# Gathers of expert passes issued one pass at a time, behind small VectorE copies of their row numbers

## The chip, the cores and the metric

The kernel runs on one core of a Trainium2 chip. Its time is the device time of one execution in microseconds (us). Three timed runs of the kernel before gave 411.81, 412.93 and 413.04 us, a median of 412.93.

## The reference

The program is an attention block followed by a mixture of experts.

```
state = f[:, :, t, :, None] * state + einsum('bhd,bhe->bhde', k[:, :, t], v[:, :, t])
y[:, :, t] = einsum('bhd,bhde->bhe', q[:, :, t], state)        # f = sigmoid(f_logit), 768 steps
x = y.transpose(0, 2, 1, 3).reshape(3072, 384)
g = argmax(x @ w_group);  e = argmax(x @ w_expert[g])          # 4 groups x 4 experts
out[token] = softmax(group)[g] * softmax(expert)[e] * (relu(x @ w1[g, e]) @ w2[g, e])
```

The sizes are batch 4, 8 heads, 768 steps, head width 48; 3072 tokens of 384 values; 16 experts with a hidden width of 1024. All is float32. A token goes to one expert only, so the kernel must find the tokens of each expert before it can multiply them.

## The kernel before

**Attention and routing** fill the first 144 us or so. They write each token's row of 384 values, with its weight and its number (386 values, 1544 bytes), to `x_dram` in HBM, and make two tables on VectorE (DVE): `rows_p` (L338), the token numbers of the 16 expert passes, and `who`, the expert of each pass.

**The expert passes** follow, 16 of them, in the order of `PLACES`. Pass 0 and the last one take 128 tokens, the fourteen between take 230 down to 174 (`WIDTHS`), the large experts first; two "early" passes of 128 tokens each are worked in between the end of attention. For a pass the kernel does this:

- `pass_of` calls `fetch` (L399 to L405), which issues the gathers of its rows from `x_dram`: an indirect DMA of up to 128 rows each, from GpSimd's (POOL's) queue, one for a pass of 128 tokens and two for a wider one. The target `xg` has six buffers.
- The rows must be turned so that the 384 values lie along the partitions. For the wide passes `square_in` does it with 16 32x32 block transposes on DVE (L426), into one of two `xe` buffers. For passes of 128 tokens, and for pass 1 at the start, `turn_in` does it on TensorE (PE, L440), and DVE copies the result from PSUM to `xe` (L441).
- `up` multiplies by w1 on PE (`hp`, L450), and ScalarE (ACT) applies relu into `h` (L451).
- `down` multiplies by w2 (`yo`, L471 for 128 tokens, L486 for wider ones). A wide pass's result is turned back by `square_out` on DVE (L433), scaled on ACT, and scattered to the output by an indirect DMA from POOL's queue (L461) that reads the token numbers from `xg`.

The weights of a pass, two loads of 1.5 MB, are issued from SP's queue (L392) and follow the release of weight buffers, three passes ahead.

**What sets the order.** In iteration n of the main loop (L964 on), PE runs `up` of pass n + 1 and then `down` of pass n. DVE runs `square_out` of pass n - 1, then `square_in` of pass n + 2. The program's order is kept on PE, DVE, ACT and SP. POOL's order is the scheduler's choice, by its own estimate of when each instruction is ready.

**The start.** At L940 `pass_of` is called for passes 0, 1 and 2, and each iteration n calls it for pass n + 3 at its beginning. As nothing but a free `xg` buffer and `rows_p` holds a gather back, the scheduler puts the first six passes' gathers (1 + 5 x 2 = 11) in a row on POOL's queue. PE meanwhile finishes the early passes' `yo` (L471), and turns in passes 0 and 1 between the steps of `up` of pass 0 (L955 to L963).

Of the kernel before, what the change touches and what calls it, by code (L numbers as in the profile page):

```python
# [12 lines left out]
U32 = mybir.dt.uint32  # L13
# [5 lines left out]
P = 128  # L19
# [4 lines left out]
def kernel(  # L24
# [12 lines left out]
    nc = tc.nc  # L37
# [5 lines left out]
    GE = G * EG  # L43
# [8 lines left out]
    EARLY = 2  # L52
    CLOSE = NC - 3

    WIDTHS = (230, 222, 214, 212, 208, 204, 200, 196, 193, 191, 189, 186, 182, 174)
# [21 lines left out]
    def const(shape, dtype, name):  # L77
        return cp.tile(shape, dtype, tag=name, name=name)

    def bank(shape, name):  # L80
        return ps.tile(shape, FP32, tag="bank", name=name)
# [192 lines left out]
    rows_p = const([P, GE, 2], U32, "rows_p")  # L274
# [120 lines left out]
    def load_weights(pool, ap):  # L395
        e = value(ap, GE - 1)
        return load_layer(pool, e, 1), load_layer(pool, e, 2)

    def fetch(pool, rows, n, top=N, late=False):  # L399

        w = {"n": n, "pool": pool, "early": top < N, "late": late, "blocks": [(j, min(P, n - j * P)) for j in range((n + P - 1) // P)]}
        w["x"] = pool.tile([P, len(w["blocks"]), RW], FP32, tag="xg", bufs=2 if pool is ep else 6, name="xg")
        for j, m in w["blocks"]:
            nc.gpsimd.indirect_dma_start(out=w["x"][:, j, :], out_offset=None, in_=x_dram[0:1 + top, :], in_offset=bass.IndirectOffsetOnAxis(ap=rows[:, j:j + 1], axis=0))  # L404
        return w  # L405

    def room(w, shape, name):

        full = w["pool"].tile([P, shape, P if w["pool"] is ep else WIDE], FP32, tag=name, name=name)
        w[name[:2].replace("xe", "xT") + "_full"] = full  # L410
        return full[:, :, 0:w["n"]]

    def squares(w, turn):


        for k_ in range(P // SQ):
            n = sum(j * P + k_ * SQ < w["n"] for j, m in w["blocks"])
            for g in range(P // SQ):
                turn(n, k_, slice(k_ * SQ, (k_ + 1) * SQ), g, slice(g * SQ, (g + 1) * SQ))

    def square_in(w):

        w["xT"] = room(w, KO, "xe")
        x = w["x"][:, :, 0:DM].rearrange("p j (o g c) -> p j g o c", o=KO, c=SQ)
        xT = w["xT_full"].rearrange("p o (j k c) -> p j k o c", j=2, c=SQ)
        squares(w, lambda n, k_, rk, g, rg: nc.vector.transpose(out=xT[rg, 0:n, k_], in_=x[rk, 0:n, g]))  # L426

    def square_out(w):

        w["rows"] = w["pool"].tile([P, 2, DM], FP32, tag="yr", name="yr")  # L430
        y = w["rows"].rearrange("p j (o g c) -> p j g o c", o=KO, c=SQ)
        yT = w["yT_full"].rearrange("p o (j k c) -> p j k o c", j=2, c=SQ)
        squares(w, lambda n, k_, rk, g, rg: nc.vector.transpose(out=y[rk, 0:n, g], in_=yT[rg, 0:n, k_]))  # L433

    def turn_in(w):
        w["xT"] = room(w, KO, "xe")
        for j, m in w["blocks"]:
            pt = bank([P, KO, P], "xg_ps")
            for ko in range(KO):
                nc.tensor.transpose(out=pt[:, ko, 0:m], in_=w["x"][0:m, j, ko * P:(ko + 1) * P], identity=ident[0:m, 0:m])  # L440
            (nc.scalar.copy if w["early"] else nc.vector.tensor_copy)(w["xT"][:, :, j * P:j * P + m], pt[:, :, 0:m])  # L441
# [34 lines left out]
    def down(w, w2):  # L476
        n = w["n"]
        if n == P:
            for _ in down_rows(w, w2):
                pass  # L480
            return
        w["yT"] = w["yT_full"][:, :, 0:n]
        for m in range(KO):
            yp = bank([P, n], "yo")
            for fo in range(FO):
                nc.tensor.matmul(yp, lhsT=w2[:, fo, m * P:(m + 1) * P], rhs=w["h"][:, fo, :], start=(fo == 0), stop=(fo == FO - 1))  # L486
            nc.scalar.copy(w["yT"][:, m, :], yp)  # L487

    def scaled(w, settle=False):
        if w["n"] > P:  # L490
            for j, m in w["blocks"]:
                with settled(settle and j):
                    put(w, j, m, w["rows"][:, j, :])
# [414 lines left out]
    mo = main.enter_context(tc.tile_pool(name="mo", bufs=2))  # L908


    PLACES = [0] + list(range(EARLY, GE)) + list(range(1, EARLY))

    def pass_of(n):
        p = PLACES[n]
        if p < EARLY:
            return fetch(mo, rows_p[:, p, 1:2], P)
        return fetch(mo, rows_p[:, p, :], WIDTHS[p - EARLY])

    fari = const([1, 1], I32, "fari")

    def weakest():

        worst = const([P, 1], FP32, "worst")
        nc.vector.tensor_reduce(out=worst, in_=decays.rearrange("p c a n -> p (c a n)"), axis=AX, op=OP.min)
        wt = bank([1, P], "wt")
        nc.tensor.transpose(out=wt, in_=worst, identity=ident)
        far = const([1, 2], FP32, "far")
        nc.vector.tensor_reduce(out=far[:, 0:1], in_=wt, axis=AX, op=OP.min)
        nc.vector.tensor_scalar(far[:, 1:2], far[:, 0:1], math.exp(-SAFE), None, OP.is_lt)
        nc.vector.tensor_copy(fari, far[:, 1:2])  # L930

    def flags():

        nc.vector.tensor_copy(both[:, 0:1], fari)
        nc.vector.tensor_scalar(rest, b_end, 0, None, OP.is_gt)
        nc.vector.tensor_tensor(both[:, 1:2], fari, rest, OP.max)

    both = const([1, 2], I32, "both_i")
    rest = const([1, 1], I32, "rest")
    ws = {n: pass_of(n) for n in range(3)}  # L940
    ahead = {n: load_weights(wq if n % 3 == 1 else wp, who[0:1, PLACES[n]:PLACES[n] + 1]) for n in range(1, 2)}
    ahead[0] = weights[0]

# [6 lines left out]
    def run_up(n):  # L950
        for _ in up(ws[n], ahead[n][0]):
            pass
# [6 lines left out]
    next(opening)  # L959
    next(opening)  # L960
    turn_in(ws[1])
    for _ in opening:
        pass  # L963
    for n in range(GE - 1):  # L964
        w = ws[n]
        if n + 3 < GE:
            ws[n + 3] = pass_of(n + 3)
        if n == 0:
            ahead[2] = load_weights(wp, who[0:1, PLACES[2]:PLACES[2] + 1])
        past, coming = ws.pop(n - 1, None), ws.get(n + 2)  # L970
        if past and past["n"] > P:
            square_out(past)
        if coming and coming["n"] > P:
            square_in(coming)
        if n + 2 < GE:
            run_up(n + 1)
        if past:

            scaled(past, n == GE - 3)
        if coming and coming["n"] == P:  # L980
            turn_in(coming)
        w["yT_full"] = outs[n % 2]
        down(w, ahead.pop(n)[1])
        if n + 3 < GE:
            ahead[n + 3] = load_weights(wq if n % 3 == 1 else wp, who[0:1, PLACES[n + 3]:PLACES[n + 3] + 1])
        if n == 2:
            with tc.tile_pool(name="tb", bufs=1) as tb:
                beyond(False, tb)
        if n == 3:
            weakest()  # L990
            flags()
# [79 lines left out]
    with tc.If(more > 0), ExitStack() as late:  # L1071
# [3 lines left out]
        mo = late.enter_context(tc.tile_pool(name="mo2", bufs=2))  # L1075
# [49 lines left out]
```

## Time and profile before

| What | us |
|---|---|
| timed runs, median of three | 412.93 |
| the profiled execution's own time | 417.84 |
| its span, first to last instruction | 416.0 |
| PE busy | 404.0 |
| DVE busy | 264.3 |
| ACT busy | 162.2 |
| POOL busy | 85.7 |

The mean granted clock of PE was 0.994 of full speed. In the views of the profile, a line of the chain or of a timeline begins with the start and the length in us; L450 is line 450 of the kernel; `out<-in` are the names of the tiles; a bracket gives the engine's idle time ahead of the group and what ended it. POOL's span of an indirect DMA is the issuing, not the transfer. PE's matmuls are pipelined and their ends are modelled.

### The profile page before, as it was taken

Reading aid. Unit: us, or ns where it says so; the run is one execution under the profiler, and the core shown is the slowest. Engines: PE = TensorE matmul, PEld = TensorE weight load, DVE = VectorE, ACT = ScalarE, POOL = GpSimd, SP = SyncE. Lnnn points to the kernel's source line nnn. Section 1 sums busy time; section 2 is a strip of 40 time slices with the busy share of each in tenths; the row PEclk is TensorE's granted clock in tenths of the full one; section 3 lists DMA queues with packets and bytes.
Section 4 is the critical chain, followed back from the end, with each engine's and each line's share of the span. In section 5 each row is a group of like instructions: output and inputs, shape, how many; then the busy total and the mean of one; then the engine's idle time right before and its main releaser. Section 6 shows DMA issues by size and latency. Waiting matters only on the chain.

```text
span 416.0 us, 10268 instructions
## 1 busy us (share of the span) xinstructions
PE 404.0 (97%) x4143; PEld 371.9 (89%) x4143; DVE 264.3 (64%) x783; ACT 162.2 (39%) x365; POOL 85.7 (21%) x132
## 2 busy tenths in 40 slices
PE   8999999999999997999999999999999999999994
PEld 3888888888888966989999999999999999999992
DVE  6666878787998702440799767485595595584230
ACT  6777878887664211211223122222231232232220
POOL 5000010101040174001041221311321230120230
PEclk9999999999999999999999999999999999999999
DMA  9999987879869499855729467586495596485010
GB/s 191 208 216 197 201 179 147 164 159 289 244 225 378 163 337 345 318 179 184 271 84 335 137 245 265 164 315 208 170 348 169 217 352 200 173 318 162 28 48 24
DMA packets 132146, 88.99 MB, mean 214 GB/s; under 512 B 102582, under 2 KB 122748, under 8 KB 132090
## 3 DMA queue, kind: packets, MB, share of 16 engines
q1 hardware_dynamic: 125666, 75.50, 60.6%
q0 software_dynamic: 5792, 11.92, 9.5%
q10 hardware_dynamic: 632, 0.83, 0.6%
q8 instruction: 35, 0.57, 0.6%
q14 instruction: 21, 0.17, 0.1%
HBM read 78.71 MB, written 9.83 MB: 213 GB/s over the span
## 4 chain that ended last, share of the span: by engine, by line
PE 48%; issue 30%; DMA 9%; POOL 6%; DVE 3%; POOLq 1%; another core or an unknown queue 1%; ACT 1%; SPq 0%; ACTq 0%; DVEq 0%
PE hp L450 12%; PE yo L486 6%; DMA out_dram<-yt,xg 6%; PE yo L471 4%; PE cs L616 4%; POOL out_dram L461 4%; PE ap L704 3%; PE y L746 3%; POOL xg L404 2%; PE x_ps L795 2%; PE tr_q L650 2%; PE tr_k L650 2%; PE y L742 2%; PE ap L689 2%; PE y L754 2%
## 5 line engine op out<-in xcount | busy, mean ns | idle before, releaser
L450 PE MATMUL hp<-xe,w 128*128 128x128 f32 (+14 forms) x864 | 141.3, 323 | 2.6 <-issue 1.8
L450 PEld LDWEIGHTS hp<-xe,w 128*128 128x128 f32 x864 | 137.4, 192 | 4.5 <-issue 2.4
L486 PE MATMUL yo<-h,w 128*128 128x230 f32 (+13 forms) x672 | 115.8, 333 | 0.0
L433 DVE STREAM_TRANSPOSE yr<-yT 32x192 f32<-32x192 f32 (+1 forms) x208 | 70.5, 339 | 70.5 <-ACT yT L487 67.9
L486 PEld LDWEIGHTS yo<-h,w 128*128 128x128 f32 x672 | 113.7, 190 | 0.2
L451 ACT ACTIVATE h<-hp 128x256 f32<-128x256 f32 (+14 forms) x72 | 34.2, 478 | 109.1 <-PE hp L450 100.2
L426 DVE STREAM_TRANSPOSE xe<-xg 32x192 f32<-32x192 f32 (+1 forms) x208 | 69.6, 335 | 8.7 <-PE hp L450 5.8
L461 POOL DMA_INDIRECT out_dram<-yt,xg x32 | 34.5, 1078 | 156.1 <-ACT yt L458 150.5
L487 ACT COPY yT<-yo 128x230 f32<-128x230 f32 (+13 forms) x42 | 13.5, 325 | 80.5 <-PE yo L486 80.5
L404 POOL DMA_INDIRECT xg<-x_dram,rows_p x30 | 29.6, 986 | 51.1 <-DMA out_dram<-yt,xg 25.7
L471 PE MATMUL yo<-w,h 128*128 128x384 f32 x64 | 21.3, 486 | 0.0
L707 DVE TENSOR_TENSOR am<-ap,tri 128x512 f32<-128x512 f32 x24 | 15.1, 688 | 7.3 <-PE ap L704 7.3
L616 PE MATMUL cs<-ld_f,tri 128*128 128x384 f32 x48 | 18.5, 505 | 0.5 <-POOL blank L177 0.3
L471 PEld LDWEIGHTS yo<-w,h 128*128 128x128 f32 x64 | 11.9, 190 | 7.4
L458 ACT ACTIVATE yt<-yr,xg 128x384 f32<-128x384 f32 (+13 forms) x26 | 14.4, 604 | 5.4 <-DVE yr L433 5.4
L623 POOL DMA_DIRECT2D ends<-eq x10 | 5.4, 542 | 52.2 <-ACT eq L617 52.2
L692 DVE TENSOR_TENSOR am<-ap,seen 128x384 f32<-128x384 f32 x24 | 12.2, 551 | 5.5 <-PE ap L689 5.5
L757 ACT COPY xT<-y 128x512 f32<-128x512 f32 x24 | 13.4, 587 | 5.0 <-PE y L746 4.4
L651 ACT COPY Tk<-tr_k 128x512 f32<-128x512 f32 x24 | 15.2, 636 | 0.0
L651 ACT COPY Tq<-tr_q 128x512 f32<-128x512 f32 x24 | 15.0, 625 | 0.4 <-PE tr_q L650 0.3
L441 DVE COPY xe<-xg_ps 128x384 f32<-128x384 f32 (+1 forms) x4 | 2.1, 535 | 20.5 <-remote 9.7
L650 PE MATMUL tr_q<-ident,qh 128*128 128x128 f32 x96 | 14.5, 274 | 0.5 <-issue 0.5
(187 smaller groups left out, 448.4 us busy)
## 6 DMA issues: line engine op xcount, KB each, us to landing
w<-in_moe_w_dram SPq DMA_DIRECT2D x34, 1536.0 KB, 7.2
qh<-in_q_dram SPq DMA_DIRECT2D x12, 384.0 KB, 6.1
ld_k<-in_k_dram SPq DMA_DIRECT2D x12, 384.0 KB, 4.4
v<-in_v_dram SPq DMA_DIRECT2D x12, 384.0 KB, 5.4
ld_f<-in_f_logit_dram SPq DMA_DIRECT2D x11, 384.0 KB, 5.5
x_dram<-x_kept SPq DMA_DIRECT2D x2, 1536.0 KB
x_dram<-x POOLq DMA_DIRECT2D x2, 384.0 KB
x_dram<-x ACTq DMA_DIRECT2D x2, 384.0 KB, 7.4
```

The source lines that it names most:

```text
L404: nc.gpsimd.indirect_dma_start(out=w["x"][:, j, :], out_offset=None, in_=x_dram[0:1 + top, :], in_offset=bass.IndirectOffsetOnAxis(ap=rows ...
L426: squares(w, lambda n, k_, rk, g, rg: nc.vector.transpose(out=xT[rg, 0:n, k_], in_=x[rk, 0:n, g]))
L433: squares(w, lambda n, k_, rk, g, rg: nc.vector.transpose(out=y[rk, 0:n, g], in_=yT[rg, 0:n, k_]))
L450: nc.tensor.matmul(hp[:, o, :], lhsT=w1[:, ko, (f + o) * P:(f + o + 1) * P], rhs=w["xT"][:, ko, :], start=(ko == 0), stop=(ko == KO - 1))
L451: nc.scalar.activation(h[:, f:f + 2, :], hp, AF.Relu)
L461: sent = nc.gpsimd.indirect_dma_start(out=out, out_offset=bass.IndirectOffsetOnAxis(ap=w["x"][0:m, j, DM + 1:RW].bitcast(U32), axis=0), in ...
L471: nc.tensor.matmul(yp, lhsT=w["h"][:, fo, :], rhs=w2[:, fo, :], start=(fo == 0), stop=(fo == FO - 1))
L486: nc.tensor.matmul(yp, lhsT=w2[:, fo, m * P:(m + 1) * P], rhs=w["h"][:, fo, :], start=(fo == 0), stop=(fo == FO - 1))
L616: nc.tensor.matmul(cs.rearrange("t h d -> t (h d)"), lhsT=tri, rhs=nl[:, b], start=True, stop=True)
L650: nc.tensor.transpose(out=pt[:, a, :], in_=w[nm + "h"][:, b, 2 * a:2 * a + 2, :].rearrange("t r d -> t (r d)"), identity=ident)
L651: nc.scalar.copy(w["T" + nm][:, b], pt)
L707: nc.vector.tensor_tensor(am[:, r], ap[r], tri.unsqueeze(1).broadcast_to((P, HP, P)), OP.mult)
```

## The change

A new constant tile `rows_next` has the shape of `rows_p`. For every pass after the second, `pass_of` first has DVE copy the pass's row numbers (128 partitions x 2) from `rows_p` to `rows_next`, and the gathers read them from there. A gather therefore waits for a DVE copy that stands in DVE's program order. The calls are also placed later: pass 2's after the turning in of pass 1, and pass n + 3's after `square_in` of pass n + 2 instead of at the start of the iteration.

```
+    rows_next = const([P, GE, 2], U32, "rows_next")
     def pass_of(n):
         p = PLACES[n]
+        if n > 1:
+            nc.vector.tensor_copy(rows_next[:, p, :], rows_p[:, p, :])
         if p < EARLY:
-            return fetch(mo, rows_p[:, p, 1:2], P)
-        return fetch(mo, rows_p[:, p, :], WIDTHS[p - EARLY])
+            return fetch(mo, (rows_next if n > 1 else rows_p)[:, p, 1:2], P)
+        return fetch(mo, (rows_next if n > 1 else rows_p)[:, p, :], WIDTHS[p - EARLY])
...
-    ws = {n: pass_of(n) for n in range(3)}
+    ws = {n: pass_of(n) for n in range(2)}
...
     turn_in(ws[1])
+    ws[2] = pass_of(2)
     for _ in opening:
         pass
     for n in range(GE - 1):
         w = ws[n]
-        if n + 3 < GE:
-            ws[n + 3] = pass_of(n + 3)
...
         if coming and coming["n"] > P:
             square_in(coming)
+        if n + 3 < GE:
+            ws[n + 3] = pass_of(n + 3)
```

In the built program POOL's queue is then: the gathers of passes 0 and 1 (three), the two clearings of `yT`, the outputs of the two early passes, the gathers of passes 2, 3 and 4, the output of pass 0, and from there on the two gathers of a pass and the outputs of an earlier one in turn. On DVE the fourteen copies stand behind the `xe` copies of pass 1 and then behind each `square_in`. The order of the instructions on PE, ACT and SP is the same as before.

## The prediction

> **What bounds the kernel now.** I read the page's busy table first, then the chain that ended last, then the timelines of the three engines that the change touches, then the windows around it.
>
> ```profile
> span 416.0 us, 10268 instructions
> PE 404.0 (97%) x4143; PEld 371.9 (89%) x4143; DVE 264.3 (64%) x783; ACT 162.2 (39%) x365; POOL 85.7 (21%) x132
> ```
>
> PE is busy for 404.0 of 416.0 us, so whatever does not reach PE is worth nothing. The moved gathers are on POOL (21%) and the new copies on DVE (64%), neither of them the bound. The question is where PE is not fed. The chain over 150 to 200 us shows the one place in the expert part:
>
> ```profile
> 154.90 2.68 PE hp L450 x24
> 157.57 0.64 PE xg_ps L440 x6
> ...
> 158.36 0.39 ACT h L451
> 158.75 4.46 another core or an unknown queue
> ...
> 163.23 0.94 ACT h L451 x3
> ...
> 164.32 11.24 PE hp L450 x48
> 175.56 5.16 PE yo L471 x16
> 180.72 9.00 PE hp L450 x48
> ```
>
> After 180.72 the chain is PE without a gap. Before it stands a hole of 4.46 us that no queue explains. It falls inside POOL's burst:
>
> ```profile
> 144.72 1.02 POOL L404 DMA_INDIRECT xg<-x_dram,rows_p  x1 [4.43 <-ACT h L451]
> 146.05 0.99 POOL L404 DMA_INDIRECT xg<-x_dram,rows_p  x1 [0.30 <-issue]
> 147.34 0.95 POOL L404 DMA_INDIRECT xg<-x_dram,rows_p  x1 [0.30 <-issue]
> 148.59 0.95 POOL L404 DMA_INDIRECT xg<-x_dram,rows_p  x1 [0.30 <-issue]
> ...
> 157.98 0.95 POOL L404 DMA_INDIRECT xg<-x_dram,rows_p  x1 [0.30 <-DMA xg<-x_dram,rows_p]
> 159.23 1.02 POOL L461 DMA_INDIRECT out_dram<-yt,xg  x1 [0.30 <-issue]
> ```
>
> Eleven gathers go out from 144.72 to 157.98, one each 1.25 us, and two outputs behind them. The trace's semaphore records say when they land: the first 6.5 us after its issue, the eighth to eleventh 8.9 to 9.1 us. Only the first three (passes 0 and 1) are needed soon. The windows, with columns PE, PEld, DVE, ACT, POOL busy, clock, DMA share, GB/s:
>
> ```profile
> 152.00:158.00 6.00, 6.00 (x41) 4.89 (x41) 0.56 (x1) 0.58 (x1) 4.48 (x6) 1.00 1.02 331
> 158.00:164.30 6.30, 3.70 (x26) 2.98 (x25) 1.02 (x3) 1.32 (x4) 2.96 (x3) 1.00 1.02 338
> 164.30:181.00 16.70, 16.68 (x67) 13.99 (x68) 10.55 (x31) 2.46 (x5) 0.00 (x0) 0.90 0.65 249
> ```
>
> In 158 to 164.3 the DMA engines are full, PE works 3.70 of 6.30 us, and afterwards PE's clock is 0.90 of full. The last view is DVE's timeline:
>
> ```profile
> 163.28 0.94 DVE L441 COPY xe<-xg_ps 128x384 f32<-128x384 f32 x2 [9.67 <-remote]
> 164.14 5.70 DVE L426 STREAM_TRANSPOSE xe<-xg 32x192 f32<-32x192 f32 x16
> 175.60 5.71 DVE L426 STREAM_TRANSPOSE xe<-xg 32x192 f32<-32x192 f32 x16 [5.76 <-PE hp L450]
> ```
>
> The copies of pass 1 wait with PE; the transposes of pass 2 start at once, at 164.14, as their rows have long been there. This is what the change takes away.
>
> [...] in 158 to 164 us the gathers' queue takes 47.9% and the weights' queue 54.2% of the engines. [...] half clock for 3.41 us from 164.9. [...]
>
> **The change, part by part.**
>
> *Removed from 148 to 159 us:* eight gathers of 128 rows of 1544 bytes, 1.6 MB, and 8 x 1.25 = 10 us of POOL's queue. What the hole costs: PE could have gone on after the transposes of 157.41 to 158.0 with the 24 records of hp left to pass 0, at 0.112 us each (2.68 us for 24 in the chain), so pass 1 could start at about 160.8 instead of 164.32: 3.5 us. Half clock for 3.41 us costs another 1.7 us, which agrees with 11.24 us for pass 1's 48 records against 9.00 x 230/222 = 9.3 us. Together 5.2 us. Taken away whole, the profiled execution's own 417.84 us (span 416.0 and 1.84 around it) would be 412.6. The median of the timed runs is already 412.93, 4.9 below the profiled execution. So either the hole is absent from timed runs, or it is in them and the 4.9 us are profiling cost of another kind. Lower bound of the gain 0, upper bound 5.2 us. I take half, 2.7, as likeliest value where there is a gain[...].
>
> *Added: 14 copies* of 128x2 row numbers on DVE. The nearest row is the cast that makes row numbers, 0.18 us for 128x32. 14 x 0.18 = 2.5 us over 230 us, one per pass. They hide in DVE's wait for PE's results: 4.3 to 5.3 us in every pass from the sixth on. Without that cover they would cost 0.2 us a pass. In passes 2 and 3 DVE has no such gap (it goes from 199.54 to 231.6 unbroken); there the transposes for pass 5 end at 231.32, and PE needs them at 233.95. Three copies add 0.5: still hidden.
>
> *Moved: the gathers of pass 2.* They now wait for a DVE copy behind the copies of pass 1 and, on POOL, stand behind the two early outputs, whose rows ACT finishes at 150.0 and 155.5, so these do not hold them. With the hole gone, pass 1's copies end at about 159.1; copy and semaphore 0.5, first gather 1.3, so the second is issued at 160.9. It must land, then come 5.7 us of transposes, and pass 2 starts on PE at 160.8 + 9.4 + 5.2 = 175.4. Room for landing: 175.4 - 5.7 - 160.9 = 8.8 us. Gathers of the trace under full DMA took 6.4 to 8.0 us where no burst stood ahead. Margin about 1 to 2 us, the narrowest of the change. If the hole stays, the margin is similar: copies end 164.2, second gather at 166.0, room 180.6 - 5.7 - 166.0 = 8.9.
>
> *Pass 3:* its copy follows pass 2's transposes (about 174.7), the second gather goes at 176.5, lands by 184.5, transposed by 190.2, needed at 175.4 + 9.0 + 9.3 = 193.7. *Pass 4:* issued at 191 to 192, landed by 200; its transposes stand behind pass 1's output transposes until 199.5 anyway. *Later passes:* a gather goes out after the previous pass's input transposes and is used one period (15 to 17.5 us) less those 5.7 us later; with 2 us of issue and 7 to 8 us to land it is there 1 to 2 us before DVE asks, and DVE itself is 4 to 5 us ahead of PE.
>
> *POOL's queue behind the new wait:* the output scatters of a pass now stand behind gathers that wait for DVE; they go 2 to 4 us later (output 0 about 9 us later). Nobody waits: four output buffers, six gather buffers. In return POOL no longer waits for the scatters to land (25.7 us in 7 waits), which PE never saw. SP's weight loads keep their places; they share the engines with 1.6 MB less until 165 us. The last gather is before 380 us and the final scatters keep their order, so the tail is as it was.
>
> Sum: copies 0, moved gathers 0, hole -2.7 (0 to -5.2).
>
> **The rivals.** *No change in timed runs.* For it: 412.6 computed without the hole is almost the 412.93 measured, and everything else is hidden. Against it: the hole lies where eleven gathers meet full weight traffic; 147 to 149 us, with weight traffic alone, and all later stages with pairs of gathers have none. Time 412.9, give or take 1. *Slower by a late pass 2.* In place of the hole, PE waits before pass 2 for rows that were gathered too late. It decides when the second gather takes over 8.8 us to land; every us above is one lost. For it: 8.9 to 9.1 us were seen at the burst's end. Against it: that was with seven gathers queued ahead, here one. With 12 us, +3.2: 416.1, if nothing is won. *The hole moves* to where pass 2's two gathers meet weight traffic: as much lost as won, or a little more, 412 to 415.
>
> **How the numbers follow.** Gain at least in part 0.48, at 410.2 (407.7 to 411.7); nothing measurable 0.36; late pass 2 0.10; moved hole 0.06, evenly over the outcomes. The 0.3% bound is 1.2 us, also the distance between the three timed runs. That gives faster 0.50, same 0.37, slower 0.13. The range reaches from the whole hole gone, 407.5, to a pass 2 late by a little, 414.0.
>
> **What would show it.** Right: POOL shows three gathers, then pairs a period apart; the 4.46 us of an unknown queue and the 0.90 clock near 160 are gone; pass 1's hp starts near 161 and pass 2's follows pass 0's yo without a gap. The after profile losing 4 to 5 us while the timed median stays says that the hole was the recording's. Wrong: a wait of DVE's transposes for a gather with PE idle before pass 2, or a hole elsewhere.

## The result, and the profile after

| | before | after |
|---|---|---|
| timed runs, median (us) | 412.49 (411.81 to 413.04, 6 runs) | 415.68 (414.03 to 416.42, 6 runs) |
| ratio after / before, 95% interval | | 1.0076 (1.0059 to 1.0092) |
| profiled execution's own time; span | 417.84; 416.0 | 415.52; 413.7 |
| rows_p ready (L338), us into the span | 142.7 | 145.8 |

The changed kernel is 0.8% slower, and the prediction (410.2 us, 407.5 to 414.0) missed it in direction and range. The profiled executions alone say the opposite, since the one of before has the hole of 4.46 us in it. Both halves of this have to be explained: a loss that the prediction did not have, and a gain that these timed runs do not show. One fact is needed for the second: chips differ (the runs below have the kernel before at 412.1 to 412.6 us on three of them and at 417.4 to 417.8 on three others), and what follows says which chip a run was on where it matters.

The page of the kernel after begins:

```profile
span 413.7 us, 10285 instructions
PE 403.1 (97%) x4143; PEld 371.3 (90%) x4143; DVE 266.9 (65%) x797; ACT 162.8 (39%) x365; POOL 86.6 (21%) x132
```

The instruction counts of PE, ACT and POOL are those of before; DVE's 14 more are the copies. The hole is gone. The chain of after over 140 to 200 us (start, length, what) is PE work without a gap:

```profile
157.98 2.68 PE hp L450 x24
160.66 0.59 PE xg_ps L440 x6
161.25 12.02 PE hp L450 x72
173.27 5.16 PE yo L471 x16
178.43 9.00 PE hp L450 x48
187.43 9.32 PE yo L486 x48
```

POOL's timeline of after shows the new order, three gathers, the two early outputs, then pairs:

```profile
150.44 0.95 POOL L404 DMA_INDIRECT xg<-x_dram,rows_p  x1 [0.30 <-issue]
...
153.39 1.02 POOL L461 DMA_INDIRECT out_dram<-yt,xg  x1 [1.22 <-ACT yt L458]
158.88 0.99 POOL L461 DMA_INDIRECT out_dram<-yt,xg  x1 [4.46 <-ACT yt L458]
162.31 0.98 POOL L404 DMA_INDIRECT xg<-x_dram,rows_next  x1 [2.44 <-DVE rows_next L918]
163.60 0.98 POOL L404 DMA_INDIRECT xg<-x_dram,rows_next  x1 [0.30 <-issue]
175.74 0.95 POOL L404 DMA_INDIRECT xg<-x_dram,rows_next  x1 [11.17 <-DVE rows_next L918]
```

And DVE's timeline of after shows what the new wait costs DVE:

```profile
161.02 0.94 DVE L441 COPY xe<-xg_ps 128x384 f32<-128x384 f32 x2 [4.33 <-PE xg_ps L440]
161.88 0.16 DVE L918 COPY rows_next<-rows_p 128x2 uint32<-128x2 uint32 x1
169.56 5.71 DVE L426 STREAM_TRANSPOSE xe<-xg 32x192 f32<-32x192 f32 x16 [7.53 <-DMA xg<-x_dram,rows_next]
175.31 0.17 DVE L918 COPY rows_next<-rows_p 128x2 uint32<-128x2 uint32 x1
180.35 5.71 DVE L426 STREAM_TRANSPOSE xe<-xg 32x192 f32<-32x192 f32 x16 [4.88 <-DMA xg<-x_dram,rows_next]
```

DVE now waits 7.53 us for the rows of pass 2 and 4.88 us for those of pass 3. Neither reaches PE: pass 2's transposes end at 175.3, and `hp` of pass 2 begins at 178.43, right behind pass 0's `yo`. So the part that was changed works as it was meant to, and the loss is not in it. It is complete before the first changed instruction: `rows_p`, from which the gathers of the 16 passes take their row numbers, is ready 3.1 us later. The first line is of before, the second of after:

```profile
L338 DVE CAST rows_p<-got x1: 180/180/180, 142.7 to 142.7; 128x32 uint32<-128x32 f32 x1
L338 DVE CAST rows_p<-got x1: 182/182/182, 145.8 to 145.8; 128x32 uint32<-128x32 f32 x1
```

Part 3 (queue, packets, MB, share of the 16 engines' span; q1 is SP's queue, which carries the loads) and part 6 (median us from issue to landing, last number) of the page of before:

```profile
q1 hardware_dynamic: 125666, 75.50, 60.6%
...
qh<-in_q_dram SPq DMA_DIRECT2D x12, 384.0 KB, 6.1
ld_k<-in_k_dram SPq DMA_DIRECT2D x12, 384.0 KB, 4.4
v<-in_v_dram SPq DMA_DIRECT2D x12, 384.0 KB, 5.4
ld_f<-in_f_logit_dram SPq DMA_DIRECT2D x11, 384.0 KB, 5.5
```

and of after:

```profile
q1 hardware_dynamic: 125666, 75.50, 67.1%
...
qh<-in_q_dram SPq DMA_DIRECT2D x12, 384.0 KB, 6.8
ld_k<-in_k_dram SPq DMA_DIRECT2D x12, 384.0 KB, 6.1
v<-in_v_dram SPq DMA_DIRECT2D x12, 384.0 KB, 7.2
ld_f<-in_f_logit_dram SPq DMA_DIRECT2D x11, 384.0 KB, 6.6
```

The same 125666 packets with the same 75.50 MB keep the engines busy for 67.1% of the span instead of 60.6%, and the attention's four loads, which nobody touched, land 0.7 to 1.8 us later.

What could an edit of the expert stage do to the loads of the attention stage? It adds a tile. `rows_next` takes 16 x 2 x 4 = 128 bytes of every SBUF partition and is allocated ahead of nearly everything else, so all later tiles move up by 128 bytes. In the built program of before, the first of the tiles `v` is at byte 162336 of its partition, which is 32 past a multiple of 256; in after it is at 160 past one. The `qh` tiles move in the same way. Their rows are 192 bytes long and 256 apart. At 32 a row covers 32 to 224 of a block of 256 bytes; at 160 it runs from 160 to 352 and crosses the block's end. That a row across the block's end makes its packet longer was at this point the author's guess; the runs and the packets' durations below test it.

### The profile page after: what moved, and what is told of

Its sections match the earlier page's. It is cut to its first block, busy times and chain, and to the rows that moved or that the text cites. A ratio compares the mean times of both kernels' runs of the same rounds, so it can differ in the third digit from the quotient of the medians.

```text
span 413.7 us, 10285 instructions
## 1 busy us (share of the span) xinstructions
PE 403.1 (97%) x4143; PEld 371.3 (90%) x4143; DVE 266.9 (65%) x797; ACT 162.8 (39%) x365; POOL 86.6 (21%) x132
## 3 DMA queue, kind: packets, MB, share of 16 engines
q1 hardware_dynamic: 125666, 75.50, 67.1%
## 4 chain that ended last, share of the span: by engine, by line
PE 81%; issue 7%; DMA 3%; DVE 3%; POOL 2%; ACT 1%; POOLq 1%; SPq 0%; DVEq 0%; ACTq 0%
PE hp L450 29%; PE yo L486 23%; PE yo L471 4%; PE cs L616 3%; PE y L746 3%; PE ap L704 2%; PE y L754 2%; PE x_ps L795 2%; PE tr_k L650 2%; PE ds L722 2%; PE ap L689 2%; PE y L742 2%; DMA ld_f<-in_f_logit_dram 2%; PE tr_q L650 2%; DMA ld_k<-in_k_dram 2%
## 5 line engine op out<-in xcount | busy, mean ns | idle before, releaser
L450 PE MATMUL hp<-xe,w 128*128 128x128 f32 (+14 forms) x864 | 138.6, 320 | 0.0
L450 PEld LDWEIGHTS hp<-xe,w 128*128 128x128 f32 x864 | 135.8, 190 | 0.8
L426 DVE STREAM_TRANSPOSE xe<-xg 32x192 f32<-32x192 f32 (+1 forms) x208 | 69.7, 335 | 15.3 <-DMA xg<-x_dram,rows_next 12.4
L404 POOL DMA_INDIRECT xg<-x_dram,rows_next x27 | 26.5, 981 | 156.5 <-DVE rows_next L918 128.5
L461 POOL DMA_INDIRECT out_dram<-yt,xg x32 | 35.6, 1111 | 39.4 <-ACT yt L458 30.8
L256 POOL DMA_DIRECT2D x_dram<-meta x6 | 4.7, 791 | 48.2 <-DVE table L266 20.2
```

Source lines behind the costliest of these rows:

```text
L450: nc.tensor.matmul(hp[:, o, :], lhsT=w1[:, ko, (f + o) * P:(f + o + 1) * P], rhs=w["xT"][:, ko, :], start=(ko == 0), stop=(ko == KO - 1))
L461: sent = nc.gpsimd.indirect_dma_start(out=out, out_offset=bass.IndirectOffsetOnAxis(ap=w["x"][0:m, j, DM + 1:RW].bitcast(U32), axis=0), in ...
```

## The experiments

*Theory A:* the 128 bytes make the rows of `v` and `qh` cross multiples of 256, their packets take longer, the loads come later, and PE is starved in the attention stage. *Rival B:* the copies, the waits or the later gathers cost the time. *Rival C:* any shift of the tiles does.

**An unused tile in the kernel before, of 128 or 256 bytes per partition; the changed kernel with 128 more.** In the first two, the line stands just ahead of `pass_of`, where the change puts `rows_next`:

```
+    const([P, 32], FP32, "pad")        # before_pad128; before_pad256 has [P, 64]
```

> The kernel before with an unused constant of 128 bytes per partition allocated where rows_next stands in the changed kernel; no instruction is added, moved or changed. It moves every later tile by 128 bytes, so the 192-byte rows of the v and q loads begin at 160 instead of 32 past a multiple of 256 bytes and cross it. Theory A (the loss is this shift: longer packets of the input loads in the attention stage): as slow as the changed kernel, 415 to 416 us, ratio 1.007; rows_p is made at about 145.8 us instead of 142.7, and the SP queue takes about 100% instead of 85% of the DMA engines up to 142 us. Theory B (the later gathers and the waits behind the copies cost it): as the kernel before, 412.5 us, ratio 1.000.

Measured: 416.52 us, ratio 1.0096 (1.007 to 1.0121).

> The same with 256 bytes per partition, so that every later tile keeps its place modulo 256. Theory A: ratio 1.000, 412.5 us. Theory B: ratio 1.000 too. If any shift costs something, whatever its size (theory C: addresses, or chance in the layout), it is slower than before by 2 to 3 us.

Measured: 412.12 us, ratio 0.9996 (0.9982 to 1.001).

```
     rows_next = const([P, GE, 2], U32, "rows_next")
+    const([P, 32], FP32, "pad")        # after_pad128
```

> The changed kernel with another 128 bytes per partition behind rows_next, so that the later tiles stand 256 bytes further than before and keep their place modulo 256; the gathers, the copies and their order are those of the changed kernel. Theory A: back at 412.5 us, ratio 0.998 to 1.002, rows_p at 142 to 143 us. Theory B: as slow as the changed kernel, 415.7 us, ratio 1.007. If the hole of 4.46 us is in timed runs of the kernel before and goes with the burst, it is faster than before, down to 407.5.

Measured: 412.48 us, ratio 0.9997 (0.9983 to 1.0011).

An unused tile alone makes the whole loss, and a second one takes it away from the changed kernel, where `rows_p` is ready at 142.6 us again. B and C fall. The kernel before took 412.27 us beside these (27 runs), so the order of the gathers by itself is worth nothing there.

The changed kernel with and without the 128 bytes makes the best pair of traces: the same instructions in the same order. Busy time by stretch, with columns PE, PEld, DVE, ACT, POOL, clock, DMA share (over 1.00 is to be read as full), GB/s. With the 128 bytes, `v` and `qh` at 32:

```profile
0.00:20.00 20.00, 18.29 (x203) 12.54 (x204) 13.73 (x39) 13.21 (x26) 6.10 (x45) 1.00 0.96 190
20.00:60.00 40.00, 39.57 (x854) 33.55 (x853) 28.42 (x75) 32.05 (x70) 3.09 (x6) 1.00 0.98 196
60.00:100.00 40.00, 40.00 (x964) 34.70 (x963) 31.68 (x88) 33.06 (x76) 4.02 (x8) 1.00 0.84 173
```

Without them (the kernel after), `v` and `qh` at 160:

```profile
0.00:20.00 20.00, 17.46 (x197) 11.58 (x198) 12.68 (x37) 12.63 (x25) 5.87 (x45) 1.00 1.06 173
20.00:60.00 40.00, 39.38 (x852) 33.29 (x851) 28.72 (x74) 31.68 (x71) 3.08 (x6) 1.00 1.15 182
60.00:100.00 40.00, 38.48 (x884) 33.33 (x884) 30.14 (x87) 31.97 (x74) 4.00 (x8) 1.00 1.12 178
```

DMA goes from 0.84 to 1.12 in 60 to 100 us at about the same GB/s, and PE loses 0.8, 0.2 and 1.5 us in the three stretches, 2.5 of the 3.1 us between the spans (410.6 and 413.7). How a late load reaches PE is seen in the chain of after over 37 to 50 us:

```profile
40.01 7.10 DMA ld_f<-in_f_logit_dram
...
47.60 0.95 DVE qh L636
48.55 0.87 DVE kh L639
```

For 7.10 us the chain is a load of `f`; in the other kernel it is PE work throughout these 13 us. The waits of DVE on loads in after, 0 to 145 us (total, times, longest), are

```profile
DVE ld_f L597 <- DMA ld_f<-in_f_logit_dram: 3.0, 4, 1.3
DVE kh L639 <- DMA ld_k<-in_k_dram: 1.5, 2, 1.1
DVE qh L636 <- DMA qh<-in_q_dram: 0.9, 1, 0.9
```

against 1.5, 0.4 and none in the other.

**Only `v` and `qh` moved; only `v`; only `eq` and `kh`.** In each, 128 unused bytes ahead of the set and 128 behind it, so that nothing else changes its place relative to 256:

```
     for nm, count in (("v", 4), ("eq", 2), ("qh", 3), ("kh", 3)):
+        if nm in ("v", "qh"):          # or ("v",), or ("eq", "kh")
+            kept([P, 32], f"ahead_{nm}")
         pads[nm] = [kept([P, 2, H, DP], f"{nm}{i}") for i in range(count)]
+        if nm in ("v", "qh"):
+            kept([P, 32], f"behind_{nm}")
```

> The kernel before with 128 unused bytes ahead of and behind the v tiles and the qh tiles: v and qh alone move by 128 bytes modulo 256 (to 160), all other tiles keep their place modulo 256. Theory A: as slow as the changed kernel, ratio 1.006 to 1.009, with v and q landing later by 1 to 2 us at the median. If other tiles (f and k loads, weights, gathered rows) carry the loss, ratio below 1.003.

Measured: 416.31 us, ratio 1.0096 (1.007 to 1.0122). The two sets of tiles are the whole cause. In this kernel's page the share of q1 and the landing times are those of after:

```profile
q1 hardware_dynamic: 125666, 75.50, 67.4%
...
qh<-in_q_dram SPq DMA_DIRECT2D x12, 384.0 KB, 7.5
ld_k<-in_k_dram SPq DMA_DIRECT2D x12, 384.0 KB, 6.1
v<-in_v_dram SPq DMA_DIRECT2D x12, 384.0 KB, 7.1
```

> The kernel before with unused bytes ahead of and behind v alone, so that v's rows cross a multiple of 256 bytes and qh's don't. Boundary theory: half of the descriptors that crossed more in the run that moved both, so about half of its cost if cost goes with their number: 413.5 to 415 us, q1 near 64.5%. Rival, only lateness of the load that is waited for counts, and nobody waits for v: 412.3 us with q1 up all the same. Rival, v carries it all: 416 us.

Measured: 413.71 us, ratio 1.0037 (1.0024 to 1.0051), q1 64.1%. No wait for the load of `v` is shown in this run, yet it costs 1.5 us. The other loads land later too, `qh` after 5.9 us and `ld_k` after 5.7, against 5.0 and 4.9 in `before_pad256`, beside a mean of 17.0 ns for a packet of 192 bytes here and 15.3 in before; that `v`'s slower packets hold up the other loads is an inference. Half of the rows costs less than half of the time. From 72 to 93 us the page's DMA digits (tenths) are 8 and 7 here and 9 and 9 in after, so the engines may have had room left; that this is the reason is not shown.

> The kernel before with 128 unused bytes ahead of and behind eq and kh, the two sets of padded tiles that ScalarE writes and no load does; v and qh keep 32 mod 256. Boundary theory, which is one of loads: nothing, 412.3 us, ratio 0.998 to 1.002, q1 61 to 62%. Rival, the engines pay for the place of their operands as well: 413 us or more, with longer ScalarE and VectorE rows on eq and kh.

Measured: 412.23 us, ratio 0.9997 (0.9985 to 1.0008), q1 61.7%. With the tiles at 160 that only engines write and read, the time stays (412.23 us beside 412.56). It is a matter of the loads.

**Smaller shifts: what is it in the place?** The unused tile of `before_pad128`, with 32 and with 64 bytes, puts the rows at 64 (they end at 256 and do not cross) and at 96 (they cross by 32 bytes):

```
+    const([P, 8], FP32, "pad")         # before_pad32; before_pad64 has [P, 16]
```

> The kernel before with an unused tile of 32 bytes per partition ahead of everything the two stages allocate: v and qh start at 64 mod 256, so their rows of 192 bytes fill the last three quarters of a 256-byte block (64 to 256) and just don't cross its end. Boundary theory (what costs is a row that crosses a multiple of 256 bytes): 412.3 us, ratio 0.998 to 1.002, q1 near 61 to 62% of the span. Rival, every move away from the place of before costs in proportion: about a quarter of the 4.2 us, 413.3 us. Rival, 64-byte alignment within the row gains something: below 411.5 us.

Measured: 412.31 us, ratio 0.9994 (0.9984 to 1.0004).

> The same with 64 bytes: v and qh start at 96 mod 256, and each of their rows has its last 32 bytes in the next block. ld_f and ld_k, whose rows of 192 bytes follow one another, start at 0 mod 256 and cross as often as before. Boundary theory: the row that crosses by 32 bytes costs like the one that crossed by 96: 415 to 417 us, ratio 1.006 to 1.012, q1 at 66% or more. Rival, in proportion to the move: about 414.4 us. Rival, the place of the tiles of f and k matters as much: under 414 us, since they begin on a boundary here.

Measured: 415.72 us, ratio 1.0077 (1.0062 to 1.0092), q1 68.0%.

Rows that just fit cost no time (0.9994), and rows that cross by 32 bytes cost about as much (1.0077) as rows that cross by 96 (1.0096). Rows that start on a multiple of 64 and cross were tried next: the sets `v` and `qh` at 192, with 40 words ahead and 24 behind in place of 32 and 32.

```
-            kept([P, 32], f"ahead_{nm}")
+            kept([P, 40], f"ahead_{nm}")
...
-            kept([P, 32], f"behind_{nm}")
+            kept([P, 24], f"behind_{nm}")
```

> The kernel before with v and qh moved to 192 mod 256: every one of their rows crosses a multiple of 256 bytes, as 64 bytes and 128, but begins on a multiple of 64. The rows of f and k, a part of which crossed from such a place in before, took 15 ns a packet like the others, and padding them gained nothing. If it takes both, a crossing and a start off the multiples of 64: 412.3 us, ratio 0.998 to 1.002, q1 near 62%, 15 ns a packet. If any crossing costs where rows stand apart (v and qh have 64 unused bytes between rows, f and k none): 415.5 to 416.5 us, q1 66% or more, 19 to 20 ns a packet.

Measured: 416.39 us, ratio 1.0094 (1.0077 to 1.0112), q1 67.0%. For `v` and `qh` the crossing decides: with their rows at 96, 160 and 192 the ratios are 1.0077, 1.0096 and 1.0094, with them at 32 (`before_pad256`) and 64 (`before_pad32`) 0.9996 and 0.9994.

**The other two loads, and a faster kernel?** Half of the rows of `f` and `k` cross a multiple of 256 in before: they are 192 bytes long and follow one another without a gap. If crossing cost there too, padding them to 256 bytes would gain.

```
-                    w[nm] = sb.tile([P, 2, H, D], FP32, tag="ld_" + nm, bufs=3 if nm == "f" else 2, name="ld_" + nm)
+                    w[nm] = sb.tile([P, 2, H, DP], FP32, tag="ld_" + nm, bufs=3 if nm == "f" else 2, name="ld_" + nm)[:, :, :, DP - D:DP]
...
-            nl = w["f"].rearrange("p b h d -> p b (h d)")
+            nl = w["f"]
...
-                nc.tensor.matmul(cs.rearrange("t h d -> t (h d)"), lhsT=tri, rhs=nl[:, b], start=True, stop=True)
+                nc.tensor.matmul(cs, lhsT=tri, rhs=nl[:, b], start=True, stop=True)
```

This is the edit for `f` and `k` together, in `before_f_k_rows`; ScalarE and TensorE read `f` with the gap. `before_k_rows` has the first pair of lines for `k` alone, and `after_f_k_rows` has the whole edit on top of `after_pad128`.

> The kernel before with the rows of ld_k padded from 192 to 256 bytes and starting on a multiple of 256, so that none of k's rows crosses; in before two of every four do. Nothing else changes its place mod 256. Boundary theory: a cut of q1's share, about a quarter of what moving all of v and q added (half as many rows of one tensor instead of all rows of two: 5 points of the span by 1/4, so 1 point less, near 60.5%), and 0 to 1 us of time, 411.3 to 412.3 us. Rival, loads aren't late enough in before for anything to be gained: 412.3 us with the lower share. Rival, strided rows in k cost VectorE: over 413 us.

Measured: 411.99 us, ratio 0.9988 (0.9977 to 0.9999), q1 61.7%.

> The kernel before with the rows of ld_f and ld_k both padded from 192 to 256 bytes and starting on a multiple of 256, so that no row of any of the four loads crosses one; ScalarE's exp and ln, VectorE's floor and the triangular matmuls read f with a gap of 64 bytes between heads. Boundary theory: the gain of padding k alone (0.6 us) about twice over: 411.0 to 412.0 us, and less waiting of VectorE on ld_f before 140 us (1.4 to 2.5 us in the kernels whose v and qh do not cross). Rival, the lateness of the loads is used up once v and qh don't cross: 412.3 us. Rival, the strided read of f by TensorE or ScalarE costs more than it saves: over 413 us, seen in the mean duration of the L616 and L607 rows.

Measured: 412.09 us, ratio 0.9996 (0.9985 to 1.0008), q1 61.8%.

> The changed kernel with 128 unused bytes behind rows_next (which puts v and qh back at 32 mod 256), and f and k padded as in the run beside it. Boundary theory: the same time as that run within 0.3%, since the order of the gathers was worth nothing with v and qh in place: 411.0 to 412.0 us. Rival, the order of the gathers is worth something once the first stage is quicker: 0.5 us or more under the run beside it.

Measured: 411.99 us, ratio 0.9999 (0.9991 to 1.0008), q1 62.1%.

Nothing is gained that the second and third of these runs confirm. The expectation was wrong in its premise: the rows of `f` and `k` that cross were not slow. The trace has the duration of every packet. The mean over all 98312 packets of 192 bytes, and the share that took over 15 ns (nearly all others took 15):

```
kernel               v, qh at (mod 256)    mean ns    over 15 ns
before               32                    15.3        1.1 %
before_f_k_rows      32                    15.4        1.0 %
after_pad128         32                    15.4        1.2 %
before_pad32         64                    16.3       11.6 %
before_k_gap_192     32                    16.4       10.9 %
before_fp_v          v 160, qh 32          17.0       16.2 %
before_pad64         96                    19.9       42.2 %
before_pad128        160                   18.9       35.4 %
before_fp_v_qh_192   192                   19.2       37.8 %
before_fp_vq         160                   19.5       38.6 %
after                160                   19.2       38.1 %
```

`v` and `qh` are half of these packets, and 35 to 42% of all turn slow when all of their rows cross. In after the price is 3.9 ns on the mean. Spread over the 16 engines, an estimate, that is 98312 x 3.9 / 16 = 24 us more per engine in a stage of 140 us, and the times rise by 3 to 4 us. How the crossing divides a row does not set the price: a row at 96 has 32 bytes in the second block, one at 160 has 96 and one at 192 has 128, and the packets take 19.9, 18.9 to 19.5 and 19.2 ns. Nor is a crossing enough by itself: half of the rows of `f` and `k` cross in before, and only 1.1% of all packets are slow.

Does the gap between rows make the difference? This run puts `k`'s rows apart like `v`'s, and across the multiple; against `before_k_rows` it changes

```
-sb.tile([P, 2, H, DP], FP32, tag="ld_" + nm, bufs=2, name="ld_" + nm)[:, :, :, DP - D:DP]
+sb.tile([P, 2, H, DP], FP32, tag="ld_" + nm, bufs=2, name="ld_" + nm)[:, :, :, 0:D]
```

> The kernel before with the rows of ld_k 256 bytes apart, as v's and qh's are, and filled from 192 mod 256, so that all of k's rows cross a multiple of 256 bytes, as 64 bytes and 128. It differs from the run that padded k in the 64 bytes between (there rows start at 0). If the gap between rows decides (f's and k's rows that cross without a gap took 15 ns): what moving v alone cost, since the number of rows is the same, 413.5 to 414 us, a little more as VectorE waits for k, up to 414.5; q1 at 64%, about a fifth of the packets of 192 bytes over 15 ns. If it is something in the tiles v and qh themselves: 412.0 us, as in the run that padded k.

Measured: 418.82 us, beside 417.44 for the kernel before on this chip; ratio 1.0028 (1.001 to 1.0046); q1 62.7%. The time is a weak witness here, as the kernel before alone spreads from 415.2 to 419.9 us on this chip; the packets are a better one. Slow packets go from 0.8% (`before_k_rows`) to 10.9%. So rows of `k` too become slow when they stand apart and cross, but fewer than those of `v` (16.2%). And `before_pad32`, where `f` and `k` start at 224 and three of four rows cross off the multiples of 64 without a gap, has 11.6% slow packets as well, at no loss of time. Which of its loads they belong to was not separated. If they are those of `f` and `k`, the gap is part of the answer and not all of it; why the abutting rows of before are spared is open.

**The hole.** That last run was on another chip (chip 6), where the kernel before took 417.44 us in 27 timed runs instead of 412.1 to 412.6 as on chips 1, 3 and 11. Its profile has the hole again. The chain of before_k_gap_192:

```profile
158.33 0.63 PE xg_ps L440 x6
...
159.10 0.38 ACT h L451
159.49 4.48 another core or an unknown queue
...
165.08 9.56 PE hp L450 x48
174.64 5.16 PE yo L471 x16
179.80 9.00 PE hp L450 x48
```

None of the profiles of the twelve kernels tried above has it, though ten of these kernels issue the same burst of eleven gathers. The granted clock of the timed runs points the same way: 0.990 to 0.997 for the kernel before on chip 6, 0.995 to 1.000 on chips 1, 3 and 11. So the hole might belong to some chips, timed runs included, and then the gain that the prediction looked for would be found there. The changed kernel and its padded version were therefore taken to more chips.

> The changed kernel with 128 unused bytes behind rows_next once more, looked at for the hole of 4.5 us that stands at the end of the burst of eleven gathers in the profiled execution of the kernel before, and again in the run with k's rows apart, beside which the kernel before took 417.44 us instead of 412.1 to 412.6. If the hole is a thing of the chip, and the burst makes it: where the kernel before takes about 417.4 us beside this run, this kernel takes about 412.5 (0.987 to 0.990), and its profile shows no stretch of an unknown queue near 160 us; where the kernel before takes 412.3, both are the same (0.998 to 1.002). If the hole comes whatever the order of the gathers: 1.000 beside either, and the hole in this profile too where the kernel before is slow.

Measured, on chip 11: 411.96 us, ratio 0.9992 (0.9979 to 1.0005), beside 412.61, and no hole in its chain; nothing new.

> The changed kernel as it is. If the chip has the hole in the kernel before (about 417.4 us there) and the moved gathers take it away: 415.7 us, ratio 0.994 to 0.998, what the hole cost less what the crossing rows cost. If they don't: 420.5 us, ratio 1.006 to 1.010. On a chip without the hole: 415.7 beside 412.4, 1.006 to 1.010.

Measured, on chip 2: 415.57 us beside 417.82, ratio 0.9939 (0.9919 to 0.9959). Here the same change makes the kernel faster. The chain of this run:

```profile
158.56 2.68 PE hp L450 x24
161.24 0.59 PE xg_ps L440 x6
161.83 12.02 PE hp L450 x72
173.85 5.16 PE yo L471 x16
```

Where before_k_gap_192 stands still behind `xg_ps`, this runs on.

> The changed kernel with v and qh put back at 32 mod 256, looked at for a chip that has the hole. If the gain from the moved gathers and the loss from the crossing rows add up: 412.4 us beside 417.4 to 417.8, ratio 0.985 to 0.989, where the chip has the hole; 412.4 beside 412.4, 0.998 to 1.002, where it hasn't. If the two don't add up (the hole comes back when the first stage ends earlier): above 0.992 where the kernel before takes 417.4 or more.

Measured, on chip 7: 411.92 us beside 417.75, ratio 0.9866 (0.9841 to 0.9892), and no hole in its chain. The two effects add up. The kernel before was not profiled on chips 2 and 7, so its hole there is inferred from the time and from the clock (0.989 to 0.997):

| | chips 1, 3, 11 (no hole) | chips 2, 6, 7 (hole) |
|---|---|---|
| before | 412.1 to 412.6 | 417.4 to 417.8 |
| after | 415.7 (chip not recorded) | 415.57 |
| after with 128 bytes more | 411.96, 412.48 | 411.92 |

The last row is the version to keep: it is level with before on the first kind of chip, 1.3% faster on the second, and faster than the changed kernel on both.

## Why the prediction was wrong, step by step

- **"Added: 14 copies", "copies 0": the step that failed.** The instructions do cost nothing: 0.16 to 0.17 us each, hidden. But they need `rows_next`, and nowhere was it asked where that tile lies and what it moves. The term of the tile was put at nothing, without a reason; it cost 3.2 us in the result, and the kernel before with an unused tile of the same size loses 4.2 us (1.0096; 412.27 to 416.52). That nothing ahead of the first changed line could change was assumed without being said.
- **"hole -2.7 (0 to -5.2)".** Both ends came true, each on its kind of chip, the lower one not for the reason given: 0 on chips 3 and 11 (0.9997, 0.9992), and 417.75 - 411.92 = 5.8 us on chip 7, where the working gave 5.2. The half between them is right nowhere. The page had the sign of it: a profiled execution of 417.84 beside timed runs of 412.93, which was read as either a cost of profiling or a hole that timed runs lack; the half taken between the two was the author's estimate, and no run showed it. It fits a profile from a chip of the second kind with timed runs from the first, though the chip of that profile is not known. That the hole is the recording's own does not fit: kernels were profiled on both kinds of chip, and the hole goes with the chip. The sign named for it would have misled: the profiled execution of `after_pad128` is 5.4 us below that of before (412.42 and 417.84) with the timed median unchanged, most likely because the two profiles come from different kinds of chip.
- **The working of the hole** (pass 1 held up, half clock after it) held. In after, pass 1 joins pass 0 without a gap. The 72 records of `hp` from 161.25 on are the 24 left to pass 0 and the 48 of pass 1, so pass 1 starts 2.68 us later, at 163.9. In `after_pad128`, where the shift of 3.1 us is gone, they start at 158.00, and pass 1 at 160.7; 160.8 was foreseen. The moved gathers take the hole away, as predicted. The half clock (3.41 us in the trace of before) is not a fixed part of it: in before_k_gap_192 the 48 records of pass 1 take 9.56 us after the hole and not 11.24, at a granted clock of 1.00. What halves it is not shown. On chip 6, timed runs of the kernel before at a mean clock of 0.996 or 0.997 have a median of 416.0 us (9 runs), and those at 0.990 one of 418.6 (4 runs). PE did not stand still throughout the hole: the 24 records left to pass 0 ran between 158.0 and 163.6 us of before, with pauses.
- **"Moved: the gathers of pass 2".** The second gather was issued at 163.60 and landed 5.8 us later, against a room of 8.8; the transposes are done 3.2 us before PE asks. The rival with a late pass 2 did not happen, and the moved hole did not either. Pass 3's second gather landed after 3.2 us where 8 were reckoned with.
- **"Nobody waits" for the late output scatters, SP's weight loads in place, the tail as it was:** `after_pad128` against before leaves room for 0.1% at most, 0.9997 (0.9983 to 1.0011).
- **The rival "no change in timed runs"** was right for the order of the gathers on chips without the hole. No rival named the side effect of the allocation, and slower had 0.13. Two sums are slightly off, and nothing hangs on them: half of 5.2 is 2.6, and the chances as described give 0.50, 0.38 and 0.12.

## What to carry to other kernels

A diff that adds a tile has a second part that no line shows: compare the addresses of all tiles in the two built programs, relative to 256 bytes, above all those that loads fill in short separate rows (here 192 bytes, 256 apart: 4.2 us of 412), and pad the new tile until they are back in place. When a loss begins before the first changed instruction, look at the queues' shares for the same packets and bytes (here 60.6% and 67.1%). And when the profiled execution and the timed runs lie 1% apart, price the stretch that differs at its two ends, as two cases, not at the half.

## What was not expected of the hardware

- Packets of 192 bytes into SBUF took 15.3 ns on average in before, with `v` and `qh` inside blocks of 256 bytes, and 18.9 to 19.9 ns in the kernels with both across their ends. A crossing by 32 bytes was about as dear (19.9 ns) as one by 96 (18.9 to 19.5).
- In before, rows that follow one another without a gap were spared: half of those of `f` and `k` cross, and 1.1% of the packets are slow. In `before_pad32` 11.6% are, and whose they are was not separated.
- One program takes 412.3 us on three chips and 417.6 us on three others. The two traces with the difference in them show a hole of 4.5 us in which ACT and DVE stand and PE works with pauses (3.70 of 6.30 us in the window of before) while the DMA engines are full (1.02 there, 1.00 in before_k_gap_192). It goes with the burst of gathers: the kernels without it had no hole on chips 2 and 7. Chips 2, 6 and 7 were each used once here, so a lasting property of the chip and its state at that time are not told apart. What the engines wait for, and what differs between the chips, the trace does not name, and it stays open.
